# Retention followed by a snake feed-forward layer on one core: the third tile's mask, mix and copies in two halves, VectorE's small tables placed later, the fourth tile turned one piece later

## The chip, the core and the metric

The kernel runs on one core of a Trainium2 chip. The metric is the device time of one execution in microseconds (us), lower is better. Several runs of a kernel are given as a median with the lowest and the highest.

The engines are called as in the profile: PE is TensorE (matrix products; PEld is its loading of weights), DVE is VectorE, ACT is ScalarE, POOL is GpSimd, SP is SyncE, which here only issues transfers. DMA transfers are issued by POOL (loads) and SP (transposes and stores) and run beside all engines.

## The reference

Two parts. The first is a retention layer: for every batch (4) and head (8) a 64 x 64 state is decayed and added to at each of 768 steps, and read with the query. The second is a feed-forward layer on the 3072 resulting rows of 512, with the snake function between its two products.

```python
for t in range(S):
    state = gamma[None, :, None, None] * state + einsum('bhd,bhe->bhde', k[:, :, t], v[:, :, t])
    y[:, :, t] = scale * einsum('bhd,bhde->bhe', q[:, :, t], state)
x = y.transpose(0, 2, 1, 3).reshape(B * S, H * D)       # 3072 x 512
h = x @ w_in                                            # 512 -> 2048
s = sin(alpha * h)
out = (h + s * s / (alpha + 1e-9)) @ w_out              # 2048 -> 512
```

## The kernel before, in words

**Tiles.** The 768 steps are cut into 6 chunks of 128. A tile is one chunk of one batch with all 8 heads, so there are 24 tiles. `order` (called `P` further down, L557) puts the first chunk of each of the four batches first; these four tiles are e0, e1, e2 and e3 (L558). They need no state of an earlier chunk. Then come the other chunks, batch by batch: P[4] and P[5] are the second and third chunk of the first batch. The tiles are gathered in 11 groups: the first has the four tiles e0 to e3 (512 rows), each other has two (256 rows).

**What a tile goes through.** It is loaded by POOL's queue, converted to bf16 on the way (L83). Stage T turns q and k on PE against an identity matrix and copies them out of PSUM into `qkT` (`stage_T`, L235; `half_T`, L222, does one of the two and is used for e0 to e2). Stage A multiplies k and q for each head into the PSUM tile `pa` and multiplies the result on DVE by a mask, into `aT` (`stage_A`, L253). For a first chunk the mask is `dec`, which holds the decay as well; for others it is `mask01`, zeros and ones, and the decay is applied by `scale_v` (to v, by the table `kg`) and by the table `qg[:, c]` of the chunk. Stage M multiplies `aT` with v into the PSUM tile `py` (L297), for a later chunk on top of the product with the state (L293), and copies it to the transposed activations `xT` of the group: ACT does it for a first chunk (L301), DVE by a product with `qg` for a later one (L304). `stage_S` (L266) adds to the state, and ACT copies it (`keep_S`, L277).

**The feed-forward layer.** 2048 hidden columns are 16 pieces of 128, called f. A `Slot` (L468) is one piece, or two, for a stretch of rows: PE multiplies `w_in` with `xT` into the PSUM tile `ph` (4 matmuls of a piece, L482), ACT takes the sine into `s` (L485), `sq` squares it on ACT ("A") or DVE ("D"), and `add` puts h + s*s/alpha into `gT` on DVE (L497, with `rec_alpha`). `ff_out` (`F` in the first group) multiplies `gT` with `w_out` (L507) into `po`, one matmul for each piece and each 128 rows.

**What sets the order.** Everything here is under a manual schedule: each engine runs its instructions in the order in which the program writes them, and waits only for the semaphores of what it reads or overwrites. PSUM tiles have tags; a tag has one buffer ("pa", "ps", "ty") or four ("mm"), and a new tile of a tag waits until the readers of the old one are done. The order around the start (L557 to L807) is written out by hand; from L808 on a table places the work of the tiles between the slots of each group.

**The first 50 us.** Loads are issued by POOL in this order: v of e0, then e1, e2, two pieces of `w_in` (four of its f each), and, behind POOL's own `scale_v(e0)` and `decay_table` 2 and 3 (L604 to L606), e3, then the pieces of `w_out` and `w_in` by turns, then P[4], P[5] and so on. `idle_work(n)` (L549) issues n matmuls of 512 columns on a tile of zeros. e0, e1 and e2 go through T, A and M. Then the first 384 rows of group 0 begin their slots, `w[0]`, `w[2]`, `w[1]`, `w[4]`, `w[7]`, `w[6]`, `w[3]`, `w[5]` (`early`, with `w[4]` in the PSUM buffer "ps"), and e3 goes through T, A and M between them. The F matmuls begin with F(1, 0, 2) (the tile e1, pieces 0 and 1), for which the first piece of `w_out` is wanted. Pieces 8 to 15 follow, then the tiles P[4] and P[5], then `phase(1, ...)`, which works on group 1 (P[4] and P[5]). From there to the end the phases follow one another.

**DVE's small tables** that the change moves: `rec_alpha` (L587, L597), `mask01` (L592), `maskq` (`later_mask`, L193: two compares on 64 partitions and a copy; first read at L359), and `qg` of the chunks 1, 4 and 5 (`decay_table`, L205; chunks 2 and 3 are POOL's).

Of the kernel before, what the change touches and what calls it, by code (L numbers as in the profile page):

```python
# [8 lines left out]
F32 = mybir.dt.float32  # L9
BF16 = mybir.dt.bfloat16  # L10
ACTF = mybir.ActivationFunctionType
ALU = mybir.AluOpType
# [3 lines left out]
def kernel(  # L16
# [15 lines left out]
    nc = tc.nc  # L32
    B, H, S, D = q.shape
    C = 128
    NCH = S // C
    NJ = B * NCH
    NP = H // 2
# [15 lines left out]
    place = {j: (g, i) for g, js in enumerate(groups) for i, j in enumerate(js)}  # L53
# [4 lines left out]
    psum = ctx.enter_context(tc.tile_pool(name="psum", bufs=1, space=bass.MemoryType.PSUM))  # L58
# [8 lines left out]
    raw = {}  # L67
# [18 lines left out]
    def wide(j):  # L86
        return j >= NCH + 2 and j % NCH > 0
# [40 lines left out]
    tio = consts.tile([128, C], F32, name="tio")  # L128
    nc.gpsimd.iota(tio, pattern=[[1, C]], channel_multiplier=0, base=0, allow_small_or_imprecise_dtypes=True)
    pos = consts.tile([128, NCH], F32, name="pos")  # L130
# [16 lines left out]
    warm = consts.tile([128, 512], BF16, name="warm")  # L147
    nc.vector.memset(warm, 0.0)  # L148
    tiny = consts.tile([128, 1], F32, name="tiny")
# [10 lines left out]
    dec = consts.tile([128, 2, NP, C], F32, name="dec")  # L160
# [12 lines left out]
    mask01 = consts.tile([128, 128], BF16, name="mask01")  # L173
    mask_bc = mask01[:, None, :].to_broadcast([128, H, 128])
# [18 lines left out]
    def later_mask():  # L193
        for b in range(2):
            nc.vector.tensor_scalar(maskq[64 * b:64 * b + 64, 0:128], tio[64 * b:64 * b + 64],
                                    tok[64 * b:64 * b + 64, 0, 0:1], None, op0=ALU.is_ge)
        nc.vector.tensor_copy(maskq[:, 128:192], maskq[:, 0:64])
# [7 lines left out]
    def decay_table(c, eng):  # L205
        eng.tensor_mul(qg[:, c], qg[:, 0], step[:, c, :, None].to_broadcast([128, NP, C]))  # L206
# [3 lines left out]
    alpha_sb = consts.tile([128, FF], F32, name="alpha_sb")  # L210
    rec_alpha = consts.tile([128, FF], F32, name="rec_alpha")
# [7 lines left out]
    st = {}  # L219
    xT = {}  # L220

    def half_T(j, i, eng):  # L222

        if i == 0:
            st["qkT", j] = work.tile([128, 2 * NP, 128], BF16, name="qkT", tag="qkT", bufs=6)
        pt = psum.tile([128, NP, 128], BF16, name="pt", tag="mm", bufs=4)
        for p in range(NP):
            nc.tensor.transpose(pt[:, p, :], raw["qk"[i], j][:, 2 * p:2 * p + 2, :].rearrange("p h d -> p (h d)"), ident)
        o = st["qkT", j][:, i * NP:(i + 1) * NP, :]
        if eng is nc.scalar:  # L230
            nc.scalar.copy(o, pt)
        else:
            nc.vector.tensor_copy(o, pt)

    def stage_T(j, eng=None, tag="ty"):  # L235
        pt = psum.tile([128, 2 * NP, 128], BF16, name="pt", tag=tag, bufs=4 if tag == "mm" else 1)
        st["qkT", j] = work.tile([128, 2 * NP, 128], BF16, name="qkT", tag="qkT", bufs=6)
        for i in range(2):
            for p in range(NP):
                nc.tensor.transpose(pt[:, i * NP + p, :],  # L240
                                    raw["qk"[i], j][:, 2 * p:2 * p + 2, :].rearrange("p h d -> p (h d)"), ident)
        if eng is nc.scalar:
            nc.scalar.copy(st["qkT", j], pt)
        else:
            nc.vector.tensor_copy(st["qkT", j], pt)
# [4 lines left out]
        nc.sync.dma_start_transpose(out=st["qkT", j], in_=raw["qk", j].rearrange(  # L250
            "i a f p d -> i (a f p d)" if wide(j) else "i a h d -> i (a h d)"))

    def stage_A(j):  # L253
        qkT = st["qkT", j]
        pa = psum.tile([128, 2, NP, 128], F32, name="pa", tag="pa")
        for p in range(NP):
            for e in range(2):
                r = slice(64 * e, 64 * e + 64)
                nc.tensor.matmul(pa[:, e, p, :], qkT[r, NP + p, :], qkT[r, p, :],  # L259
                                 start=(p == 0), stop=True, skip_group_check=True)  # L260
        aT = work.tile([128, 2, NP, 128], BF16, name="aT", tag="aT", bufs=2)
        m = dec.rearrange("p e n t -> p (e n) t") if j % NCH == 0 else mask_bc
        nc.vector.tensor_mul(aT.rearrange("p e n t -> p (e n) t"), pa.rearrange("p e n t -> p (e n) t"), m)  # L263
        st["aT", j] = aT

    def stage_S(j):  # L266
        c = j % NCH
        if c == 0:
            st["ps"] = psum.tile([128, NP, D], F32, name="ps", tag="ps")
        ps = st["ps"]  # L270
        for p in range(NP):
            for e in range(2):
                nc.tensor.matmul(ps[64 * e:64 * e + 64, p, :], raw["k", j][:, 2 * p + e, :], raw["v", j][:, 2 * p + e, :],
                                 start=(c == 0 and p == 0), stop=True, skip_group_check=True)
        return ps

    def keep_S(j, ps):  # L277
        for e in range(2):
            r = slice(64 * e, 64 * e + 64)
            nc.scalar.copy(s_bd[(j % NCH + 1) % 2][r, :, r], ps[r, :, :])  # L280

    def stage_M(j, tag="ty"):
        c = j % NCH
        g, i = place[j]
        if g not in xT:
            xT[g] = work.tile([128, KS, sizes[g] * C], BF16, name="xT", tag="xT", bufs=3)
        qkT, aT, vs = st["qkT", j], st["aT", j], raw["v", j]
        py = psum.tile([128, NP, 128], F32, name="py", tag=tag)
        if c > 0:
            for p in range(NP):  # L290
                for e in range(2):
                    r = slice(64 * e, 64 * e + 64)
                    nc.tensor.matmul(py[r, p, :], s_bd[c % 2][:, p, r], qkT[:, p, :],  # L293
                                     start=(p == 0), stop=True, skip_group_check=True)
        for p in range(NP):
            for e in range(2):
                nc.tensor.matmul(py[64 * e:64 * e + 64, p, :], vs[:, 2 * p + e, :], aT[:, e, p, :],  # L297
                                 start=(c == 0 and p == 0), stop=True, skip_group_check=True)
        x = xT[g][:, :, i * C:(i + 1) * C]
        if c == 0:  # L300
            nc.scalar.copy(x, py)  # L301
            return
        ps = stage_S(j) if c < NCH - 1 else None
        nc.vector.tensor_mul(x, py, qg[:, c])  # L304
        if ps is not None:
            if wide(j + 1):
                swapped(s_b[(c + 1) % 2], ps, nc.scalar.copy)
                swapped(s_f, ps, nc.vector.tensor_copy)
            else:
                keep_S(j, ps)  # L310

    def half(x):
        return slice(64 * x, 64 * x + 64)

    def swapped(o, ps, copy):

        m = NP // 2
        copy(o[:, :m], ps[:, :m])  # L320
        for e in range(2):
            copy(o[half(1 - e), m:], ps[half(e), m:])
# [226 lines left out]
    def idle_work(n):  # L549
        for _ in range(n):  # L550
            nc.tensor.matmul(spare["ps"], warm[:, :128], warm, start=True, stop=True)  # L551

    def grow(p):
        nc.scalar.activation(out=qg[:, 0, p, :], in_=tio, func=ACTF.Exp, scale=lgp[:, p:p + 1], bias=cscale)
# [3 lines left out]
    e0, e1, e2, e3 = P[:B]  # L558
# [14 lines left out]
    grow(0)  # L573
    idle_work(2)
    stage_A(e0)
    grow(1)
    half_T(e1, 0, nc.scalar)
# [5 lines left out]
    nc.scalar.copy(alpha_sb, pal)  # L583
    stage_M(e0)
    stage_A(e1)
    idle_work(2)
    nc.vector.tensor_scalar_add(rec_alpha, alpha_sb, 1e-9)  # L587
    grow(3)
    half_T(e2, 0, nc.scalar)
    idle_work(2)  # L590
    half_T(e2, 1, nc.vector)
    nc.vector.tensor_scalar(mask01, tio, pos[:, 0:1], None, op0=ALU.is_ge)  # L592
    stage_M(e1)
    nc.scalar.activation(out=tiny, in_=warm[:, 0:1], func=ACTF.Sin)
    idle_work(1)
    stage_A(e2)
    nc.vector.reciprocal(rec_alpha, rec_alpha)  # L597
    later_mask()
    decay_table(1, nc.vector)
    idle_work(6)  # L600
    stage_M(e2)
    idle_work(3)

    scale_v(e0, nc.gpsimd)  # L604
    decay_table(2, nc.gpsimd)
# [54 lines left out]
    def F(ts, lo, hi):  # L660
        for f in range(lo, hi):
            ff_out(0, ts, f)

    def early(f, tag="mm"):
        return Slot(0, f, (0, n3), tag=tag)

    w = {}
    decay_table(4, nc.vector)
    w[0] = early(0)
    w[0].sq("D")  # L670
    w[2] = early(2)
# [5 lines left out]
    w[1].add()  # L677
    w[7] = early(7)
    w[2].add()
    stage_T(e3, nc.vector, "ty")  # L680
    w[7].sq("A")
    w[6] = early(6)
    decay_table(5, nc.vector)
    w[6].sq("A")
    stage_A(e3)
    w[4].sq("A")
# [77 lines left out]
    F(1, 8, 9)  # L764
    w[13].sq("A")
    w[10].add()
    F(0, 6, 8)
    w[14] = Slot(0, 14)
    F(2, 0, 1)
# [4 lines left out]
    F(0, 9, 10)  # L774
    w[14].sq("A")
    w[13].add()
    F(0, 10, 12)
    w[15] = Slot(0, 15)
    F(2, 2, 3)
    w[12].add()  # L780
    w[14].add()
    w[15].sq("A")
    F(2, 3, 4)
    F(2, 4, 6)
    F(0, 12, 13)
    stage_T(P[4], nc.vector, "pa")
    F(0, 13, 15)
    w[15].add()
    F(1, 10, 12)
    stage_A(P[4])  # L790
    F(0, 15, 16)
# [9 lines left out]
    scale_v(P[5], nc.vector)  # L801
    F(2, 7, 11)
    stage_M(P[4])
    F(2, 11, 16)
    stage_M(P[5])
    stage_T(P[6], nc.vector, "mm")
# [66 lines left out]
```

## Time and profile before

| | |
|---|---|
| median of 3 runs | 212.47 us (211.97 to 213.03) |
| the profiled execution | 212.53 us |
| its span, first to last instruction | 210.8 us |
| granted TensorE clock | 1.000 |
| busy: PE, DVE, ACT, POOL | 200.8, 156.9, 157.4, 108.4 us |
| first slot of the feed-forward layer starts on PE | 15.29 us |
| first F matmul starts on PE | 24.01 us |
| first matmul of phase 1 starts on PE | 48.20 us |

A row of a timeline is: start in us, time it took in us, engine, line, operation, what is written and read, how many instructions of the kind were merged into the row, and, in brackets, how long the engine had been idle before it and what ended that. "L507" is line 507 of the kernel. A matmul's row ends some 0.16 us after PE has begun the next one, since the matmuls are pipelined; starts tell more than ends. A row of a DMA gives the time that POOL took to issue it; the time to landing is given apart.

### The profile page before, as it was taken

Reading aid. Unit: us, or ns where it says so; the run is one execution under the profiler, and the core shown is the slowest. Engines: PE = TensorE matmul, PEld = TensorE weight load, DVE = VectorE, ACT = ScalarE, POOL = GpSimd, SP = SyncE. Lnnn points to the kernel's source line nnn. Section 1 sums busy time; section 2 is a strip of 40 time slices with the busy share of each in tenths; the row PEclk is TensorE's granted clock in tenths of the full one; section 3 lists DMA queues with packets and bytes.
Section 4 is the critical chain, followed back from the end, with each engine's and each line's share of the span. In section 5 each row is a group of like instructions: output and inputs, shape, how many; then the busy total and the mean of one; then the engine's idle time right before and its main releaser. Section 6 shows DMA issues by size and latency. Waiting matters only on the chain.

```text
span 210.8 us, 5640 instructions
## 1 busy us (share of the span) xinstructions
PE 200.8 (95%) x2252; PEld 132.0 (63%) x2278; DVE 156.9 (74%) x348; ACT 157.4 (75%) x337; POOL 108.4 (51%) x143
## 2 busy tenths in 40 slices
PE   7998899999999999999999999999999999999994
PEld 3544554557766666667667666666666666666653
DVE  7797985777988687787797777778777768686540
ACT  7767798458998877877877877876876786888821
POOL 8898433898895929999989941000222020000000
PEclk9999999999999999999999999999999999999999
DMA  9999999999999999999999999165123110110113
GB/s 129 153 190 153 191 207 187 154 182 216 122 123 149 154 100 130 161 117 142 151 180 171 162 126 125 62 66 79 63 70 71 54 48 5 50 53 0 50 50 103
DMA packets 100282, 24.76 MB, mean 117 GB/s; under 512 B 92816, under 2 KB 97312, under 8 KB 100256
## 3 DMA queue, kind: packets, MB, share of 16 engines
q0 software_dynamic: 77504, 13.38, 93.5%
q1 hardware_dynamic: 22608, 10.96, 26.9%
q8 instruction: 18, 0.29, 0.6%
q14 instruction: 8, 0.07, 0.1%
q10 hardware_dynamic: 144, 0.07, 0.1%
HBM read 27.27 MB, written 6.29 MB: 159 GB/s over the span
## 4 chain that ended last, share of the span: by engine, by line
PE 87%; DMA 4%; POOL 3%; DVE 2%; issue 2%; ACT 1%; DVEq 0%; POOLq 0%
PE po L507 37%; PE ph L482 36%; DMA w_out<-in_moe_w_out_dram 4%; PE spare L551 3%; PE poh L532 2%; PE py L338 2%; PE py L293 1%; PE pa L259 1%; POOL qg L206 1%; PE pt L240 1%; PE pa L375 1%; PE py L420 1%; POOL qkr L83 1%; PE py L297 1%; PE pa L350 1%
## 5 line engine op out<-in xcount | busy, mean ns | idle before, releaser
L497 DVE SCALAR_TENSOR_TENSOR gT<-s,rec_alpha,ph 128x256 bf16<-128x256 f32 (+3 forms) x184 | 82.1, 489 | 31.6 <-ACT s L490 31.1
L485 ACT ACTIVATE s<-ph,alpha_sb 128x256 f32<-128x256 f32 (+3 forms) x184 | 79.4, 481 | 33.1 <-PE ph L482 32.1
L482 PE MATMUL ph<-xT,w_in 128*128 128x256 bf16 (+3 forms) x735 | 98.8, 277 | 0.1
L507 PE MATMUL po<-w_out,gT 128*128 128x512 bf16 x344 | 90.1, 379 | 4.1 <-issue 2.9
L482 PEld LDWEIGHTS <-w_in 128*128 128x128 bf16 x736 | 70.6, 98 | 30.6 <-DMA w_in<-in_moe_w_in_dram 0.5
L490 ACT ACTIVATE s<-s 128x512 f32<-128x512 f32 (+1 forms) x91 | 56.4, 623 | 2.7
L507 PEld LDWEIGHTS <-gT 128*128 128x128 bf16 x368 | 34.0, 98 | 27.0 <-issue 0.9
L391 POOL CAST s_b<-s_f 128x256 bf16<-128x256 f32 x5 | 2.0, 397 | 42.4 <-DVE s_f L384 24.9
L138 POOL TENSOR_TENSOR v_seq<-v_seq,kgq 128x512 bf16<-128x512 bf16 x14 | 14.6, 1068 | 8.8 <-DMA v_seq<-in_v_dram 8.8
L104 POOL DMA_DIRECT2D qk_seq<-in_q_dram x24 | 17.1, 748 | 2.5 <-DMA vr<-in_v_dram 0.8
L104 POOL DMA_DIRECT2D qk_seq<-in_k_dram x24 | 17.1, 734 | 0.5 <-DMA qk_seq<-in_q_dram 0.4
L519 DVE COPY o_sb<-po 128x512 f32<-128x512 f32 x19 | 13.1, 692 | 5.6 <-PE po L507 5.5
L104 POOL DMA_DIRECT2D v_seq<-in_v_dram x24 | 17.0, 754 | 0.0
L359 DVE TENSOR_TENSOR aTw<-pa,maskq 128x768 bf16<-128x768 f32 x14 | 13.3, 952 | 0.0
L551 PE MATMUL spare<-warm 128*128 128x512 bf16 x28 | 10.1, 486 | 1.4 <-DVE warm L148 1.2
L83 POOL DMA_DIRECT2D vr<-in_v_dram x10 | 9.2, 918 | 3.7 <-DMA w_out<-in_moe_w_out_dram 3.4
L138 POOL TENSOR_TENSOR vr<-vr,kg 128x512 bf16<-128x512 bf16 x8 | 8.6, 1079 | 3.2 <-DMA vr<-in_v_dram 2.6
L83 POOL DMA_DIRECT2D qkr<-in_q_dram x9 | 8.1, 897 | 3.8 <-DMA w_in<-in_moe_w_in_dram 3.6
L83 POOL DMA_DIRECT2D qkr<-in_k_dram x9 | 8.0, 889 | 3.6 <-DMA w_out<-in_moe_w_out_dram 3.1
L443 DVE TENSOR_TENSOR xT<-py,qg 128x256 bf16<-128x256 f32 x26 | 9.7, 416 | 0.0
L263 DVE TENSOR_TENSOR aT<-pa,mask 128x1024 bf16<-128x1024 f32 x6 | 7.3, 1218 | 0.0
L492 DVE TENSOR_TENSOR s<-s 128x512 f32<-128x512 f32 (+1 forms) x7 | 4.4, 633 | 3.7 <-ACT s L485 3.7
(108 smaller groups left out, 154.8 us busy)
## 6 DMA issues: line engine op xcount, KB each, us to landing
out_dram<-o_sb SPq DMA_DIRECT2D x23, 256.0 KB, 2.4
w_in<-in_moe_w_in_dram POOLq DMA_DIRECT2D x4, 512.0 KB, 9.7
w_out<-in_moe_w_out_dram POOLq DMA_DIRECT2D x4, 512.0 KB, 13.9
vr<-in_v_dram POOLq DMA_DIRECT2D x10, 128.0 KB, 6.6
qk_seq<-in_q_dram POOLq DMA_DIRECT2D x16, 80.0 KB, 6.1
qk_seq<-in_k_dram POOLq DMA_DIRECT2D x16, 80.0 KB, 5.1
v_seq<-in_v_dram POOLq DMA_DIRECT2D x16, 80.0 KB, 5.8
qkr<-in_q_dram POOLq DMA_DIRECT2D x9, 128.0 KB, 6.9
```

What stands on the lines that cost most here:

```text
L83: nc.gpsimd.dma_start(out=t, in_=chunk_of(src, j))
L104: nc.gpsimd.dma_start(out=o, in_=src[bt, h, cs[0] * C:, :].rearrange("(f i) d -> i f d", i=64))
L138: eng.tensor_mul(t, t, by[:, j % NCH, :, None].to_broadcast([128, H, D]))
L359: return {"mask": lambda: nc.vector.tensor_mul(aT, pa[:, :, 0:384].rearrange("p e (m t) -> p e m t", m=2), maskq[:, None, None, :].to_broa ...
L443: nc.vector.tensor_mul(x[:, 2 * b:2 * b + 2, :], y.rearrange("p (m t) -> p m t", m=2), qg[:, c, 2 * b:2 * b + 2])
L482: nc.tensor.matmul(self.ph[:, m, :], w_in[:, i, f * 128:(f + 1) * 128], xT[g][:, i, self.lo:self.hi], start=(m == 0 and i == 0), stop=(i = ...
L485: nc.scalar.activation(out=self.s[:, m, :], in_=self.ph[:, m, :], func=ACTF.Sin, scale=alpha_sb[:, f:f + 1])
L490: nc.scalar.activation(out=self.s, in_=self.s, func=ACTF.Square)
L497: nc.vector.scalar_tensor_tensor(gT[self.g][:, f, self.lo:self.hi], self.s[:, m, :], rec_alpha[:, f:f + 1], self.ph[:, m, :], op0=ALU.mult ...
L507: nc.tensor.matmul(po[g, ts], gT[g][:, f, ts * C:(ts + 1) * C], w_out[:, f, :], start=(f == 0), stop=(f == FF - 1))
L519: nc.vector.tensor_copy(o_sb, po[g, ts])
L551: nc.tensor.matmul(spare["ps"], warm[:, :128], warm, start=True, stop=True)
```

## The change

- e2's stage A is called with two parts: the eight matmuls are as before, but DVE's product with `dec` is made in two halves, one for the head pairs 0 and 1, one for 2 and 3.
- e2's stage M is replaced by `halves_M`: four matmuls into a PSUM tile with the tag "ps", copied to `xT` by ACT, two matmuls of `idle_work`, four matmuls into a tile with the tag "ty", copied to `xT` by DVE. Around it `idle_work` is 3 + 2 + 3 instead of 6 + 3.
- The dummy sine of ACT, which loads the table of sines, stands ahead of e1's stage M instead of behind it.
- On DVE, `rec_alpha` (both instructions) and `decay_table(1)` come behind e2's copies; `mask01` goes from ahead of e2's mask to behind `w[10].add()`; `decay_table(4)` and `(5)` go to behind `w[13].add()` and `w[14].add()`; `maskq` goes to behind `stage_M(P[4])`.
- `stage_T(e3)` comes behind the slot `w[6]` instead of ahead of its matmuls.
- `w[15].add()` comes ahead of `stage_T(P[4])` instead of behind it and two F matmuls.

```diff
-    def stage_A(j):
+    def stage_A(j, parts=1):
...
-        m = dec.rearrange("p e n t -> p (e n) t") if j % NCH == 0 else mask_bc
-        nc.vector.tensor_mul(aT.rearrange("p e n t -> p (e n) t"), pa.rearrange("p e n t -> p (e n) t"), m)
+        flat = "p e n t -> p (e n) t"
+        if parts > 1:
+            for h in range(0, NP, NP // parts):
+                r = slice(h, h + NP // parts)
+                nc.vector.tensor_mul(aT[:, :, r], pa[:, :, r], dec[:, :, r])
+        else:
+            nc.vector.tensor_mul(aT.rearrange(flat), pa.rearrange(flat), dec.rearrange(flat) if j % NCH == 0 else mask_bc)
...
+    def halves_M(j):
+        g, i = place[j]
+        aT, vs = st["aT", j], raw["v", j]
+        for h, (tag, copy) in enumerate((("ps", nc.scalar.copy), ("ty", nc.vector.tensor_copy))):
+            idle_work(2 * h)
+            py = psum.tile([128, 2, 128], F32, name="py", tag=tag)
+            for n in range(2):
+                for e in range(2):
+                    p = 2 * h + n
+                    nc.tensor.matmul(py[64 * e:64 * e + 64, n, :], vs[:, 2 * p + e, :], aT[:, e, p, :],
+                                     start=(n == 0), stop=True, skip_group_check=True)
+            copy(xT[g][:, 2 * h:2 * h + 2, i * C:(i + 1) * C], py)
...
     idle_work(2)
-    nc.vector.tensor_scalar_add(rec_alpha, alpha_sb, 1e-9)
     grow(3)
     half_T(e2, 0, nc.scalar)
     idle_work(2)
     half_T(e2, 1, nc.vector)
-    nc.vector.tensor_scalar(mask01, tio, pos[:, 0:1], None, op0=ALU.is_ge)
+    nc.scalar.activation(out=tiny, in_=warm[:, 0:1], func=ACTF.Sin)
     stage_M(e1)
-    nc.scalar.activation(out=tiny, in_=warm[:, 0:1], func=ACTF.Sin)
     idle_work(1)
-    stage_A(e2)
+    stage_A(e2, 2)
+    idle_work(3)
+    halves_M(e2)
+    idle_work(3)
+    nc.vector.tensor_scalar_add(rec_alpha, alpha_sb, 1e-9)
     nc.vector.reciprocal(rec_alpha, rec_alpha)
-    later_mask()
     decay_table(1, nc.vector)
-    idle_work(6)
-    stage_M(e2)
-    idle_work(3)
...
     w = {}
-    decay_table(4, nc.vector)
     w[0] = early(0)
...
     w[2].add()
-    stage_T(e3, nc.vector, "ty")
     w[7].sq("A")
     w[6] = early(6)
-    decay_table(5, nc.vector)
+    stage_T(e3, nc.vector, "ty")
     w[6].sq("A")
     stage_A(e3)
...
     w[10].add()
+    nc.vector.tensor_scalar(mask01, tio, pos[:, 0:1], None, op0=ALU.is_ge)
     F(0, 6, 8)
...
     w[13].add()
+    decay_table(4, nc.vector)
     F(0, 10, 12)
     w[15] = Slot(0, 15)
     F(2, 2, 3)
     w[12].add()
     w[14].add()
+    decay_table(5, nc.vector)
     w[15].sq("A")
     F(2, 3, 4)
     F(2, 4, 6)
     F(0, 12, 13)
+    w[15].add()
     stage_T(P[4], nc.vector, "pa")
     F(0, 13, 15)
-    w[15].add()
     F(1, 10, 12)
     stage_A(P[4])
...
     stage_M(P[4])
+    later_mask()
     F(2, 11, 16)
     stage_M(P[5])
```

## The prediction

> **What bounds the kernel now.** I read the page first (the shares, then the chain that ended last), then the timeline of PE up to 50 us, the landing of each early load, and the timelines of DVE and POOL beside them.
>
> ```profile
> span 210.8 us, 5640 instructions
> PE 200.8 (95%) x2252; PEld 132.0 (63%) x2278; DVE 156.9 (74%) x348; ACT 157.4 (75%) x337; POOL 108.4 (51%) x143
> PE 87%; DMA 4%; POOL 3%; DVE 2%; issue 2%; ACT 1%; DVEq 0%; POOLq 0%
> ```
>
> PE bounds it. The 4% of DMA is one piece: the chain has 8.49 us of the first piece of w_out, 15.47 to 23.97, ahead of the first F matmul. From there PE is on the chain nearly all the time. So there are two regions: up to 24 us (as it will turn out, 34 us) loads set the time, and afterwards PE does, with DVE at a few places.
>
> ```profile
> 14.55 0.82 PE L551 MATMUL spare<-warm 128*128 128x512 bf16 x3
> 15.29 3.67 PE L482 MATMUL ph<-xT,w_in 128*128 128x384 bf16 x20
> 19.69 0.80 PE L240 MATMUL pt<-ident,qkr 128*128 128x128 bf16 x8 [0.73 <-DMA qkr<-in_q_dram]
> 20.33 0.81 PE L482 MATMUL ph<-xT,w_in 128*128 128x384 bf16 x4
> 21.28 0.40 PE L259 MATMUL pa<-qkT 64*128 64x128 bf16 x8
> 21.61 1.47 PE L482 MATMUL ph<-xT,w_in 128*128 128x384 bf16 x8
> 23.01 0.41 PE L297 MATMUL py<-aT,vr 128*64 128x128 bf16 x8
> 24.01 1.02 PE L507 MATMUL po<-w_out,gT 128*128 128x512 bf16 x3 [0.58 <-DMA w_out<-in_moe_w_out_dram]
> ```
>
> The reader is to see PE stopped twice by a load, at 19.69 for e3's q and at 24.01 for w_out. Issue plus time to landing, asked for one load at a time, gives: w_in piece 0 7.66 + 7.2 = 14.9; piece 1 8.4 + 9.0 = 17.4 (the weight loads of PE wait 0.5 us for w_in at one place); e3's k 13.74 + 6.3 = 20.0; w_out 0 15.47 + 8.5 = 24.0; w_in 2 16.22 + 10.3 = 26.5; w_out 1 16.95 + 12.1 = 29.0; w_in 3 17.68 + 14.2 = 31.9; w_out 2 18.42 + 15.8 = 34.2; w_out 3 19.93 + 16.8 = 36.7. The pieces of 512 KB land 2.3 to 3 us apart throughout (three loads of 128 KB lie ahead of w_out 0): a full line, not a late issue, sets these times. F(1, 8, 9) is the first to need w_out 2, and PE starts it at 34.22, 0.22 us after its last slot matmul was through.
>
> **The front, part by part (11 to 34 us).** DVE loses rec_alpha (0.72) and mask01 (0.80) from between e1's product and e2's.
>
> ```profile
> 2.05 0.43 DVE L164 TENSOR_SCALAR ident<-tio,pos 128x128 bf16<-128x128 f32 x1
> 11.16 0.72 DVE L587 TENSOR_SCALAR rec_alpha<-alpha_sb 128x16 f32<-128x16 f32 x1
> 12.12 0.80 DVE L592 TENSOR_SCALAR mask<-tio,pos 128x128 bf16<-128x128 f32 x1
> 12.85 1.21 DVE L263 TENSOR_TENSOR aT<-pa,dec 128x1024 bf16<-128x1024 f32 x1
> 10.81 2.03 POOL L206 TENSOR_TENSOR qg<-qg,step 128x512 f32<-128x512 f32 x2
> ```
>
> e2's copy of k then starts when its transposes end, 11.4 instead of 11.79, stage A at 12.0 instead of 12.26, the product at about 12.45 instead of 12.85. In halves it takes more: a 512-wide product out of PSUM is 0.69 (xT<-py,qg), so two are 1.38 for 1.21, but the first is out at 13.1. Four matmuls of M follow at 13.2, two spares (0.43), then at 13.85, behind the second half, the other four. DVE's 256-wide copy, 0.4 by the 0.37 of ACT's casts of that width and DVE's 0.69 for 512, ends at 14.6; ACT's half starts once the moved table load (1.28) and e1's copy are done, 13.5, and ends earlier. The spares fall from 10 to 9, 0.22 less. PE could start the slots at 14.65 instead of 15.29. But w_in 0 lands at 14.9, so it starts there: 0.4 earlier. Then three slots (12 matmuls, 1.95 us) bring it to 16.85, and the fourth needs w_in 1, 17.4. The 0.4 is gone there. Next `w[4]`, `w[7]` and the moved `w[6]` end near 19.45; e3's turn waits for q and k as before (19.69, 20.0), its DVE copy ends at 21.2 as before, stage A starts at 21.28 as before. `w[6]` merely went from behind the turn to ahead of it: the 0.73 us wait shrinks and one of the same size opens between turn and A. decay_table(5) (0.68) leaves the gap in which DVE waits for A anyway. M(e3) at 23.0 and F at 24.01 stay. **Sum of the front: 0.** Its cover is the loads: 0.55 us at 16.85, and then 0.6 us at 24.0 and 0.2 at 34.2. If the line of loads were not there, the gain would be 0.4 to 0.65.
>
> **34 to 41 us, what comes back.** The tables land here. mask01 at 34.2 (0.3 to 0.8) and decay_table(4) at 36.1 (0.68) fit in gaps in which DVE waits for ACT (0.98 to 1.27 us each): 0. decay_table(5) does not.
>
> ```profile
> 37.16 1.41 DVE L497 SCALAR_TENSOR_TENSOR gT<-s,rec_alpha,ph 128x512 bf16<-128x512 f32 x2 [0.98 <-ACT s L490]
> 39.82 0.69 DVE L245 COPY qkT<-pt 128x1024 bf16<-128x1024 bf16 x1 [1.25 <-PE pt L240]
> 40.43 0.74 DVE L497 SCALAR_TENSOR_TENSOR gT<-s,rec_alpha,ph 128x512 bf16<-128x512 f32 x1
> 41.09 1.22 DVE L263 TENSOR_TENSOR aT<-pa,mask 128x1024 bf16<-128x1024 f32 x1
> ```
>
> Now: adds of w[12] and w[14] to 38.57, idle, copy of P[4]'s turn 39.82 to 40.52, add of w[15] 40.43 to 41.17; PE makes A(P[4]) at 40.58 and waits 0.25 us for that add, F(0, 15, 16) at 41.23. Then: decay_table(5) 38.5 to 39.2; the add of w[15] when its square is done (ACT ends it at 39.65), 39.68 to 40.43; only then the copy, 40.35 to 41.04. A(P[4]) starts at 41.10, 0.52 later, takes 0.33, and F(0, 15, 16) starts at 41.44: **+0.2**. The wait on the add is gone, a longer one on the copy is in its place. Behind it PE is dense, so the 0.2 stays; P[4]'s product, P[5]'s copy (43.4, A(P[5]) at 43.44, another 0.03) and the two scalings shift by 0.3 to 0.4 and have that cover.
>
> **46 to 48 us, maskq.** It is put between the xT products of P[4] and P[5].
>
> ```profile
> 45.41 0.69 DVE L304 TENSOR_TENSOR xT<-py,qg 128x512 bf16<-128x512 f32 x1
> 47.35 0.69 DVE L304 TENSOR_TENSOR xT<-py,qg 128x512 bf16<-128x512 f32 x1 [1.25 <-PE py L297]
> 46.45 1.09 POOL L138 TENSOR_TENSOR vr<-vr,kg 128x512 bf16<-128x512 bf16 x1
> 14.14 0.83 DVE L195 TENSOR_SCALAR maskq<-tio,tok 64x128 bf16<-64x128 f32 x2
> 15.01 0.49 DVE L197 COPY maskq<-maskq 128x64 bf16<-128x64 bf16 x1
> ```
>
> xT of P[4] ends at 46.35, xT of P[5] could start at 47.58 (47.35 + 0.23) and end at 48.27; PE, through with its turns, wants it at 48.43 (48.20 + 0.23). So the three have 1.25 us and there are 0.1 us behind them. Undisturbed they take under 0.9: nothing. But two rows above show compares that last as long as POOL's product: mask01, of the same shape as `ident`, took 0.80 against 0.43 and ended at 12.92, POOL's second qg at 12.84; rec_alpha, 16 wide, took 0.72, to 11.88, where the first qg ends. So here the second compare (from 46.55) would wait for POOL's product, which ends near 47.6; copy (0.1 to 0.49) until 47.85 to 48.2; xT until 48.55 to 48.9; PE starts 0.15 to 0.5 late. Bounds: 0, if the compares don't wait, and 1.3, if each of the three waits for a POOL instruction (below). I take **+0.3**, the middle of what those rows give for one wait.
>
> The Trainium skill, "SBUF — State Buffer", section "Who interferes with whom", says that copies and tensor_scalar in VectorE's two-port modes hold a port pair shared with GpSimd for a whole instruction, and that the later one blocks. The two rows agree; by that rule the 0.3 stands, and without it this place would cost 0 and the sum be 0.2.
>
> **Sum.** 0 + 0.2 + 0.3 = +0.5 us on the profiled execution's 212.53 us (1.7 of it outside the span): 213.0. The median shown, 212.47, is 0.06 lower, which changes nothing. After 48 us PE starts are dense to the end, so a shift there stays. A measurement of this kernel (211.97 to 213.03) tells about 0.5%, 1.06 us, from no change.
>
> **Rivals.**
> 1. maskq slips through between POOL's instructions: only +0.2, 212.75. For it: the second compare of L195 took 0.28 while POOL was issuing a load. Chance 0.2.
> 2. It gains: the loads come earlier in runs than in this profile, or w[15]'s square ends before decay_table(5) matters. Price: 0.4 of the front, or the 0.3 at 41.23; 212.0 to 212.2. Against it: execution and median agree within 0.06, and the loads are a full line. Chance 0.13. Both together would be 0.9, still under 1.06; more than that needs something I don't see, 0.04.
> 3. The other side: maskq is caught three times. POOL follows its product with issues of 0.7 us from 47.44 on; were the three to end with the product (47.6) and two issues (48.2, 48.9), xT ends at 49.6 and PE starts phase 1 1.2 late: with the 0.2, 214.0. It decides from the point where maskq's copy ends after 47.7; L197's 0.49, which ends with an issue of POOL at 15.50, speaks for it, the 0.28 above against. Chance 0.15.
> 4. PE cools. Its spares took 0.45 each at the start (3.59 for 8) and 0.22 later. The waits between 16.8 and 24 are regrouped: 0.55, 0.25, 0.95, 0.6. At half speed the 2.4 us of matmuls there and some 3 us behind would cost about 2.5: 215.0. Before has waits of 0.25, 0.75, 0.3 and 0.6 there and stays fast. Chance 0.03.
>
> The Trainium skill, "TensorE: Matmul & The Clock Gate", section "The HAM clock gate (the "warmup" mystery)", puts the fall back to half rate behind an idle window of about 3.4 us; by that rule rival 4 does not happen, as no wait here comes near it.
>
> **Chances.** Forecast 213.0 (by itself 212.7 to 213.4) 0.45; rival 1 0.2, 2 0.13, more gain 0.04, 3 0.15, 4 0.03. Faster 0.04; within 0.5% 0.45 + 0.2 + 0.13 = 0.78; slower 0.18. The range, 212.0 to 214.0, leaves out what lies beyond rivals 2 and 3.
>
> **What would show it.** Right: slots start near 14.9 and pause for w_in near 17.4; F starts at 24.0 and 34.2 as now; A(P[4]) at 41.1 behind the copy; a compare of L195 over 0.5 us at 46.5; phase 1 at 48.7. Wrong: F at 24.01 moves with the front, or phase 1 starts before 48.2.

## The result, and the profile after

The changed kernel takes 213.36 us (median of 10 runs, 212.66 to 213.74), the kernel before, in 10 runs, 212.05 us (211.81 to 213.03). The ratio is 1.0045, 95% interval 1.0028 to 1.0062: slower by 0.6 to 1.3 us. The forecast was 213.0. The profiled execution of the changed kernel took 213.03 us, 0.50 more than that of before. This 0.50 can be followed step by step; what the medians show beyond it cannot, and is taken up at the end of the experiments. The two profiled executions do not lie alike among the runs: that of before, 212.53, is longer than eight of its ten, that of the changed kernel, 213.03, shorter than seven of its ten. So the 0.50 is less than the medians differ by.

From the page of the changed kernel:

```profile
span 211.3 us, 5639 instructions
PE 200.4 (95%) x2251; PEld 132.1 (63%) x2277; DVE 157.3 (74%) x350; ACT 157.1 (74%) x337; POOL 108.2 (51%) x143
...
PE 86%; DMA 5%; POOL 3%; issue 2%; DVE 1%; ACT 1%; POOLq 0%
PE ph L501 39%; PE po L526 36%; DMA w_in<-in_moe_w_in_dram 5%; PE poh L551 2%; POOL qkr L83 2%; PE py L357 2%; POOL vr L83 1%; PE pa L259 1%; PE py L298 1%; PE pt L240 1%; PE pa L394 1%; PE pa L369 1%; PE py L439 1%; PE py L302 1%; DVE qkT L245 1%
```

PE bounds it as before. The DMA piece on the chain is now w_in instead of w_out: the second piece, issued at 8.39, landed at 18.9. The changed kernel's lines are numbered 19 higher from its `Slot` on: L501 is L482 of before, L526 is L507. Its timeline of PE, the rows that answer to those of before:

```profile
15.36 2.12 PE L501 MATMUL ph<-xT,w_in 128*128 128x384 bf16 x12 [0.26 <-DMA w_in<-in_moe_w_in_dram]
18.97 2.12 PE L501 MATMUL ph<-xT,w_in 128*128 128x384 bf16 x12 [1.48 <-DMA w_in<-in_moe_w_in_dram]
20.93 0.61 PE L240 MATMUL pt<-ident,qkr 128*128 128x128 bf16 x8
22.32 0.40 PE L259 MATMUL pa<-qkT 64*128 64x128 bf16 x8 [0.79 <-DVE qkT L245]
...
24.06 0.41 PE L302 MATMUL py<-aT,vr 128*64 128x128 bf16 x8
24.40 1.04 PE L526 MATMUL po<-w_out,gT 128*128 128x512 bf16 x3
...
34.40 0.81 PE L526 MATMUL po<-w_out,gT 128*128 128x512 bf16 x3
...
41.28 0.40 PE L259 MATMUL pa<-qkT 64*128 64x128 bf16 x8 [0.44 <-DVE qkT L245]
41.61 0.61 PE L526 MATMUL po<-w_out,gT 128*128 128x512 bf16 x2
...
48.68 1.03 PE L501 MATMUL ph<-xT,w_in 128*128 128x256 bf16 x8
```

The reader is to see four times, each against before. F(1, 0, 2) starts at 24.40 (24.01), F(1, 8, 9) at 34.40 (34.22), F(0, 15, 16) at 41.61 (41.23), phase 1 at 48.68 (48.20). So the lateness is 0.39, then 0.18, 0.38, 0.48; the end of the span is 0.50 later. Of the 0.39 a part is given back, because before waited for w_out 2 at 34.22 (it landed at 34.17 in both kernels) and the changed kernel does not. Then two additions follow, 0.20 and 0.10.

DVE around the second and the third of these, and POOL beside it:

```profile
38.67 0.68 DVE L206 TENSOR_TENSOR qg<-qg,step 128x512 f32<-128x512 f32 x1
39.87 0.75 DVE L516 SCALAR_TENSOR_TENSOR gT<-s,rec_alpha,ph 128x512 bf16<-128x512 f32 x1 [0.51 <-ACT s L509]
40.53 0.68 DVE L245 COPY qkT<-pt 128x1024 bf16<-128x1024 bf16 x1
...
45.79 0.69 DVE L309 TENSOR_TENSOR xT<-py,qg 128x512 bf16<-128x512 f32 x1
46.40 1.42 DVE L195 TENSOR_SCALAR maskq<-tio,tok 64x128 bf16<-64x128 f32 x2
47.85 0.23 DVE L197 COPY maskq<-maskq 128x64 bf16<-128x64 bf16 x1
47.94 0.69 DVE L309 TENSOR_TENSOR xT<-py,qg 128x512 bf16<-128x512 f32 x1
```

```profile
46.34 1.09 POOL L138 TENSOR_TENSOR vr<-vr,kg 128x512 bf16<-128x512 bf16 x1
```

The copy of P[4]'s turn waits for the add of w[15], and A(P[4]) for the copy. The two compares of maskq take 1.42 us together; the first alone 1.12, to 47.52, POOL's product ending at 47.43. P[5]'s xT ends at 48.63, 0.05 us ahead of phase 1.

### The profile page after: what moved, and what is told of

Its sections match the earlier page's. It is cut to its first block, busy times and chain, and to the rows that moved or that the text cites. A ratio compares the mean times of both kernels' runs of the same rounds, so it can differ in the third digit from the quotient of the medians.

```text
span 211.3 us, 5639 instructions
## 1 busy us (share of the span) xinstructions
PE 200.4 (95%) x2251; PEld 132.1 (63%) x2277; DVE 157.3 (74%) x350; ACT 157.1 (74%) x337; POOL 108.2 (51%) x143
## 4 chain that ended last, share of the span: by engine, by line
PE 86%; DMA 5%; POOL 3%; issue 2%; DVE 1%; ACT 1%; POOLq 0%
PE ph L501 39%; PE po L526 36%; DMA w_in<-in_moe_w_in_dram 5%; PE poh L551 2%; POOL qkr L83 2%; PE py L357 2%; POOL vr L83 1%; PE pa L259 1%; PE py L298 1%; PE pt L240 1%; PE pa L394 1%; PE pa L369 1%; PE py L439 1%; PE py L302 1%; DVE qkT L245 1%
## 5 line engine op out<-in xcount | busy, mean ns | idle before, releaser
L501 PE MATMUL ph<-xT,w_in 128*128 128x256 bf16 (+3 forms) x735 | 98.6, 277 | 1.8 <-DMA w_in<-in_moe_w_in_dram 1.7
L526 PE MATMUL po<-w_out,gT 128*128 128x512 bf16 x344 | 90.1, 379 | 3.2 <-issue 2.9
L501 PEld LDWEIGHTS <-w_in 128*128 128x128 bf16 x736 | 70.6, 98 | 32.5 <-DMA w_in<-in_moe_w_in_dram 2.6
L526 PEld LDWEIGHTS <-gT 128*128 128x128 bf16 x368 | 34.0, 98 | 25.8
```

The lines of the kernel that those rows point to most:

```text
L501: nc.tensor.matmul(self.ph[:, m, :], w_in[:, i, f * 128:(f + 1) * 128], xT[g][:, i, self.lo:self.hi], start=(m == 0 and i == 0), stop=(i = ...
L526: nc.tensor.matmul(po[g, ts], gT[g][:, f, ts * C:(ts + 1) * C], w_out[:, f, :], start=(f == 0), stop=(f == FF - 1))
```

## The experiments

**Theory A** is the prediction's: the front gives nothing, since loads bound it; the time is lost behind 34 us, where the copy waits for w[15] and maskq waits for POOL. **Theory B**: the front itself costs, because with `w[6]` gone from behind e3's turn PE waits for the copy of it (the 0.79 above). Its variant B2, formed after the first four runs: the new front makes w_in land late.

Single runs lie up to 0.65% below and 1% above the median of their kernel, so the edits are told apart by two lengths in the profiles: how long behind the landing of w_out 0 F(1, 0, 2) starts, and from F(1, 8, 9) to phase 1. Before has 0.04 and 13.98 us, the changed kernel 0.39 and 14.28. Much of the spread lies ahead of these lengths: F(1, 8, 9) starts 0.04 to 0.23 us behind the landing of w_out 2, and that was anywhere from 33.1 to 35.0 us. Before and "before again", the same kernel, differ by 0.69 us there and by 0.67 in their spans. "Apart" is how long behind w_in 1 the load of w_out 0 lands.

| kernel | ratio (95%) | w_in 1 lands | apart | F(1, 0, 2) behind w_out 0 | F(1, 8, 9) | phase 1 behind that |
|---|---|---|---|---|---|---|
| before | | 17.4 | 6.52 | 0.04 | 34.22 | 13.98 |
| changed | 1.0045 (1.0028 to 1.0062) | 18.9 | 5.09 | 0.39 | 34.40 | 14.28 |
| w15 back | 1.0029 (1.0011 to 1.0046) | 17.7 | 5.25 | 0.24 | 33.19 | 14.96 |
| turn back | 1.0027 (1.0007 to 1.0047) | 18.6 | 5.08 | 0.05 | 33.84 | 14.30 |
| tables back | 1.0013 (0.9995 to 1.003) | 18.2 | 5.09 | 0.39 | 33.68 | 14.18 |
| front only | 1.0022 (1.0002 to 1.0043) | 18.4 | 5.33 | 0.05 | 34.52 | 13.99 |
| three undone | 0.9994 (0.997 to 1.0017) | 18.2 | 5.08 | 0.04 | 33.45 | 13.98 |
| before, w15 first | 1.001 (0.9985 to 1.0036) | 17.3 | 5.85 | 0.04 | 33.37 | 14.18 |
| before, turn later | 1.0011 (0.9988 to 1.0033) | 17.3 | 6.33 | 0.04 | 33.79 | 13.98 |
| before, 3 spares more | 1.0048 (1.0023 to 1.0073) | 18.0 | 5.09 | 0.05 | 33.33 | 13.98 |
| before again | 0.9987 (0.9964 to 1.0009) | 18.2 | 5.08 | 0.04 | 33.53 | 13.98 |
| before, maskq late | 1.0021 (1.0001 to 1.004) | 18.2 | 6.63 | 0.04 | 35.05 | 14.23 |
| before, F swapped | 1.0003 (0.998 to 1.0026) | 16.8 | 7.54 | 0.05 | 34.55 | 13.77 |
| before, 3 spares less | 1.0001 (0.9982 to 1.002) | 17.9 | 6.07 | 0.09 | 34.12 | 13.99 |

### The changed kernel with one part undone

w15 back:

```diff
-    w[15].add()
     stage_T(P[4], nc.vector, "pa")
     F(0, 13, 15)
+    w[15].add()
```

> The changed kernel with one order undone: w[15].add() again behind P[4]'s turn and F(0, 13, 15). Theory A (VectorE's new order behind 34 us costs the time: P[4]'s copy waits for the add of w[15]): F(0, 15, 16) starts about 0.2 us earlier against the first slot matmuls before it, and the ratio to before falls from 1.0045 by 0.001 to 0.002, to about 1.003. Theory B (the front costs it: with one slot less behind the turn of e3, TensorE waits there when the second piece of w_in lands late): no change, 1.0045.

F(0, 15, 16) again starts 0.64 behind A(P[4]) with the wait of 0.25 for the add, as before, and A(P[4]) no longer waits for the copy. But phase 1 came later, not earlier. PE, DVE and POOL of this kernel ahead of it:

```profile
46.56 1.07 PE L240 MATMUL pt<-ident,qkr 128*128 128x128 bf16 x16
48.15 1.03 PE L501 MATMUL ph<-xT,w_in 128*128 128x256 bf16 x8 [0.52 <-DVE xT L309]
```

```profile
45.28 2.01 DVE L195 TENSOR_SCALAR maskq<-tio,tok 64x128 bf16<-64x128 f32 x2
47.32 0.18 DVE L197 COPY maskq<-maskq 128x64 bf16<-128x64 bf16 x1
47.41 0.68 DVE L309 TENSOR_TENSOR xT<-py,qg 128x512 bf16<-128x512 f32 x1
```

```profile
45.21 0.91 POOL L83 DMA_DIRECT2D vr<-in_v_dram  x1
46.10 1.09 POOL L138 TENSOR_TENSOR vr<-vr,kg 128x512 bf16<-128x512 bf16 x1
```

Here both compares were held: the first to 46.17, when POOL's issue of a load ended (46.12), the second to 47.29 (product 47.19). That cost 0.69 us on PE: from the first of the 16 matmuls of the turns to phase 1 it is 1.59 here and 0.90 in before (the 0.52 in brackets begins at the end of the turns' row). So maskq's price depends on what POOL does in the 2 us beside it. Another 0.27 went to P[5]'s k, not yet landed when its turn began; the edit touches no load. The ratio, 1.0029, is what theory A expected, though this execution does not show it.

Turn back:

```diff
+    stage_T(e3, nc.vector, "ty")
     w[7].sq("A")
     w[6] = early(6)
-    stage_T(e3, nc.vector, "ty")
```

> The changed kernel with one order undone: e3's turn again ahead of the slot w[6]. Theory A: the loads cover it, F(1, 0, 2) starts where it did within 0.1 us, ratio 1.0045 as the changed kernel. Theory B: the 0.79 us wait between turn and stage A is filled by the slot again, M(e3) comes up to 0.5 us earlier where w_in lands late, and the ratio falls to about 1.002.

w_in 1 landed late here too (18.6), and yet M(e3) was through in time and F(1, 0, 2) started 0.05 behind its load: theory B is right for this part. F was in time although the loads lay only 5.08 apart. In the three kernels with both the new front and the later turn (changed, w15 back, tables back) F starts 5.48 behind w_in 1, with the loads 5.09 to 5.25 apart. The rest, 14.30, is that of the changed kernel, as theory A has it. PE of this kernel:

```profile
18.60 1.47 PE L501 MATMUL ph<-xT,w_in 128*128 128x384 bf16 x8 [1.24 <-DMA w_in<-in_moe_w_in_dram]
19.91 0.78 PE L240 MATMUL pt<-ident,qkr 128*128 128x128 bf16 x8
20.53 0.81 PE L501 MATMUL ph<-xT,w_in 128*128 128x384 bf16 x4
21.48 0.40 PE L259 MATMUL pa<-qkT 64*128 64x128 bf16 x8
...
23.68 1.02 PE L526 MATMUL po<-w_out,gT 128*128 128x512 bf16 x3
```

The slot of four matmuls again lies between turn and A, and PE hardly waits for the copy.

Tables back (mask01, maskq and decay tables 4 and 5 where they were before; the rest as changed; of the edit, maskq is shown):

```diff
     nc.vector.reciprocal(rec_alpha, rec_alpha)
+    later_mask()
...
     stage_M(P[4])
-    later_mask()
```

> The changed kernel with mask01, maskq and decay tables 4 and 5 again at the places they had before; halves, spares, turn and the early add of w[15] stay. Theory A: most of the cost is the add of w[15] ahead of the copy, which stays, so it moves by 0.1 us (maskq) at most: ratio 1.004; phase 1 starts about 0.1 us earlier than with the tables late. If the tables themselves are the cost, it falls to 1.001. Theory B: no change either.

14.18: 0.10 less than the changed kernel, 0.20 more than before. The 0.20 is the add of w[15], the 0.10 maskq, as theory A had it. The time does not agree with that: theory A expected 1.004, and the ratio is 1.0013, its interval ending at 1.003, near the 1.001 that was to stand for the tables as the main cost. "Three undone" below keeps mask01 and decay tables 4 and 5 late and loses nothing, so if a table costs more over many runs than the 0.10 of this profile, it is maskq.

Front only (the kernel before with the new front, its tables, turn and add of w[15] as they were; a part of the edit, against before):

```diff
-    stage_A(e2)
+    stage_A(e2, 2)
+    idle_work(3)
+    halves_M(e2)
...
-    idle_work(6)
-    stage_M(e2)
```

> Before with the front of the change alone: halves, table load of ScalarE, 9 spares, rec_alpha and decay table 1 behind e2; turn, add of w[15] and the other tables as before. Both theories: the slots are ready earlier by up to 0.6 us, the landing of w_in takes it back, F(1, 0, 2) starts at the landing of w_out: ratio 1.000 within 0.0015. If the loads were not the limit, 0.997.

In its profile PE waits 0.60 us for w_in 0, 0.39 for w_in 1 and 0.33 for w_out 0; both lengths are those of before. So the halves gain nothing and cost nothing there. The ratio, 1.0022, is above what was expected, at most 1.0015, and its interval leaves out 1. The next run has the same front, but for the tables, and 0.9994, so this may be spread; it was not shown.

### All three undone, and single parts added to before

Three undone (the two edits above, and `later_mask` behind P[5]'s xT; new front, late mask01 and late decay tables stay):

```diff
     stage_M(P[4])
-    later_mask()
     F(2, 11, 16)
     stage_M(P[5])
+    later_mask()
```

> The changed kernel with the add of w[15] and e3's turn back at their places and maskq behind P[5]'s xT; the new front and the late mask01 and decay tables 4, 5 stay. Theory A (VectorE's order behind 34 us is the cost): ratio 1.000 to 1.001, and phase 1 starts 13.9 to 14.0 us behind F(1, 8, 9) as before. Theory B2 (something of the new front delays the loads: the second piece of w_in landed at 17.7 to 18.9 in five profiles with the new front against 17.4 before): ratio stays at 1.002 and w_in 1 lands at 17.7 or later.

Time and both lengths are those of before, and the interval lies wholly below that of the changed kernel. Within it the whole loss lies in these three places. mask01 and the decay tables, which stayed late, cost nothing.

Before, with the add of w[15] first:

```diff
+    w[15].add()
     stage_T(P[4], nc.vector, "pa")
     F(0, 13, 15)
-    w[15].add()
```

> Before with one edit: w[15].add() ahead of P[4]'s turn. Theory A: A(P[4]) about 0.5 later, F(0, 15, 16) 0.2 later, ratio 1.001; phase 1 starts 14.2 us behind F(1, 8, 9) instead of 14.0. Theory B2: ratio 1.000 to 1.001 as well, but w_in 1 lands near 17.4 with the old front.

14.18, +0.20, and the wait moves from the add to the copy:

```profile
40.24 0.40 PE L259 MATMUL pa<-qkT 64*128 64x128 bf16 x8 [0.44 <-DVE qkT L245]
40.57 0.61 PE L507 MATMUL po<-w_out,gT 128*128 128x512 bf16 x2
```

Decay table 5 is in its old place here, so it has no part in the 0.20.

Before, with e3's turn later:

```diff
-    stage_T(e3, nc.vector, "ty")
     w[7].sq("A")
     w[6] = early(6)
     decay_table(5, nc.vector)
+    stage_T(e3, nc.vector, "ty")
```

> Before with one edit: e3's turn behind the slot w[6]. Theory A: the loads cover it, ratio 1.000, F(1, 0, 2) at the landing of w_out 0. Theory B: TensorE idles 0.8 us between turn and stage A; M(e3) comes up to 0.5 later and F(1, 0, 2) up to 0.4 later where w_in lands late, ratio up to 1.002. Theory B2: w_in 1 near 17.4.

PE idled 1.07 us ahead of A(e3), and F(1, 0, 2) still started with its load, which left it 0.54 to wait: the loads lay 6.33 apart. By the 5.48 of the three kernels above, the later turn costs when they lie closer than that; this is an estimate. How late w_in 1 lands by itself does not decide it: in "w15 back" it landed at 17.7, earlier than in most, and F was 0.24 late, since w_out 0 came only 5.25 behind.

Before, with three spares more:

```diff
-    idle_work(3)
+    idle_work(6)
```

> Before with three more matmuls of idle_work (0.65 us) behind e2's stage M: the first slot is ready 0.65 later. Theory A (loads bound the front): the slots start near 15.9, w[4] at 17.9 against 17.5, and M(e3) and F(1, 0, 2) move by 0.2 at most: ratio 1.000. If TensorE bounded the front: +0.65, ratio 1.003. Theory B2: w_in 1 near 17.4.

```profile
14.48 1.47 PE L551 MATMUL spare<-warm 128*128 128x512 bf16 x6
15.79 2.11 PE L482 MATMUL ph<-xT,w_in 128*128 128x384 bf16 x12
18.07 1.47 PE L482 MATMUL ph<-xT,w_in 128*128 128x384 bf16 x8 [0.17 <-DMA w_in<-in_moe_w_in_dram]
...
23.16 1.02 PE L507 MATMUL po<-w_out,gT 128*128 128x512 bf16 x4
```

In the profile the loads take the 0.65 us in, as theory A says: the fourth slot starts with w_in 1, F 0.05 behind w_out 0, phase 1 at 47.31. What this execution lost, it lost later: from phase 1 to the end of the span it took 163.78 us, 1.22 more than before (162.56; the changed kernel 162.57), and PE waited at 57 and 81 us for v that POOL had scaled late. "Before, turn later" has 163.16 there, and a wait for such a v at 81. The ratio of 1.0048 is not what theory A expects. By this profile it need not come from the front; whether the edit brings the later waits about stays open.

Before again:

> The kernel before, unchanged, as if it were an experiment. It says how far a ratio may lie from 1 with no difference at all, and gives a second profile with the old front. Both theories: 1.000 within 0.002. Theory B2 (the new front delays the loads) wants w_in 1 near 17.4 again; if it lands at 18 or later here, the landing is chance.

w_in 1 landed at 18.2 with the old front and no edit at all, 5.08 ahead of w_out 0, so a late landing does not need the new front. That alone does not dispose of theory B2. In the six profiles with the new front w_in 1 landed at 18.3 on average and the loads lay at most 5.33 apart in every one; in the eight with the old front it landed at 17.6 on average, and they lay closer than 5.48 in two. w_out 0 itself did not land later with the new front (23.5 on average, against 23.8). Whether the new front brings the two loads together stays open. The ratio, 0.9987, shows how far one lies from 1 by itself.

Before, with maskq late (out of the front, and):

```diff
     stage_M(P[4])
+    later_mask()
     F(2, 11, 16)
```

> Before with one edit: maskq between the xT products of P[4] and P[5], as in the change. Theory A, as it now stands (a compare waits until the instruction of GpSimd that runs beside it ends): one or two of the three instructions last about 1.0 us instead of 0.28, P[5]'s xT ends 0.3 to 0.7 late, TensorE waits that long ahead of phase 1, phase 1 starts 14.3 to 14.7 us behind F(1, 8, 9); ratio 1.001 to 1.003. Rival (they slip through): 14.0 us, ratio 1.000.

DVE of this kernel, then POOL:

```profile
46.85 1.57 DVE L195 TENSOR_SCALAR maskq<-tio,tok 64x128 bf16<-64x128 f32 x2
48.45 0.18 DVE L197 COPY maskq<-maskq 128x64 bf16<-128x64 bf16 x1
48.54 0.69 DVE L304 TENSOR_TENSOR xT<-py,qg 128x512 bf16<-128x512 f32 x1
```

```profile
47.22 1.09 POOL L138 TENSOR_TENSOR vr<-vr,kg 128x512 bf16<-128x512 bf16 x1
```

The compares end behind POOL's product (48.3) again, and phase 1 starts 0.25 us later than in before, a little less than the 0.3 to 0.7 expected. Alone, maskq costs 0.25; behind the late copy of the change 0.10, since PE is late by then itself.

Before, with two matmuls swapped:

```diff
-    F(0, 15, 16)
     F(1, 12, 13)
+    F(0, 15, 16)
```

> Before with one edit: F(1, 12, 13) ahead of F(0, 15, 16), so that a matmul that needs nothing new fills the wait for the add of w[15]. The 0.25 us wait at F(0, 15, 16) shrinks to about 0.05; phase 1 starts 13.8 us behind F(1, 8, 9) instead of 14.0; ratio 0.999, hardly to be told from 1.

13.77, 0.21 shorter than before: this removes the wait that the change meant by its order of w[15]. No difference can be measured in the time (1.0003), and no version here was measurably faster than before.

Before, with three spares less:

```diff
-    idle_work(3)
```

> Before without the last three matmuls of idle_work (0.65 us): the first slot could start at 14.65. Theory A (loads bound the front): it starts when w_in 0 lands, w[4] when w_in 1 lands, ratio 1.000. If TensorE bounded the front in most executions, as the ratio 1.0048 of the kernel with three spares more may say: ratio 0.997.

The time did not change, but the test is not clean: PE then waited 0.67 us for ACT's copy of e2 and started at 15.72.

**What stays open.** The profiles account for 0.5 us, the interval asks for 0.6 to 1.3. Two of the three places differ between the profiles, maskq from 0.10 to 0.69 and the start of F from 0.24 to 0.39 in kernels with the new front and the later turn, and the ratio of "tables back" points at maskq, so a larger mean is likely; it was not shown. The stretch behind the start of phase 1 differs too, 162.55 to 163.78 us, without a known cause.

## Why the prediction held, and where it did not

- **The loads bound the front: right.** The slots were to start near 14.9 and pause near 17.4. They started at 15.36, with w_in 0 (0.26 waited), and paused until 18.97 for w_in 1. F(1, 8, 9) starts 0.23 behind the landing of w_out 2. The loads also hid that PE was ready for the slots at about 14.94 (the last spares from 14.28, 0.82 less the 0.16 by which rows overlap) instead of 14.65; the second half's matmuls started at 14.05, not 13.85. All this rests on the profiles; the ratio of "before, 3 spares more" is not explained by it.
- **"Sum of the front: 0": too low by 0.18.** The step that failed is the one on e3's turn: "`w[6]` merely went from behind the turn to ahead of it", with 0.6 us of cover at 24.0. The cover was counted from one execution, in which w_out 0 landed 6.52 us behind w_in 1. The two lay 5.08 to 7.54 apart in 14 profiles. With the later turn, turn, copy and A follow each other with no slot to fill the 0.95 between turn and A, and F started 5.48 behind w_in 1 in the three kernels with the new front and the later turn. In the changed kernel the loads lay 5.09 apart: M(e3) starts at 24.06 instead of 23.01, and F is 0.39 late, 0.18 behind 34 us. The sign that the prediction named for being wrong, that F at 24.01 moves with the front, came, with F later and not earlier.
- **The add of w[15] ahead of the copy, +0.2: right**, 0.19 to 0.20 in four kernels, by the mechanism named (a wait of 0.44 on the copy in place of 0.25 on the add).
- **maskq, +0.3: right in kind, too high in this execution.** The compare of 1.12 us beside POOL's product is there (the first of the two, not the second), so rival 1 falls. On PE it cost 0.10 in the changed kernel, 0.25 alone and 0.69 where both compares were held for long, by an issue and by the product; that is like rival 3, which had three holds. xT ended at 48.63, inside the 48.55 to 48.9 that were worked out; but PE, 0.18 later than forecast by the turn, wanted it only at 48.58 instead of 48.43. The two misses have one cause and cancel, so the sum, 0.18 + 0.20 + 0.10 = 0.48, agrees with the +0.5 better than its terms do. That is luck.
- **The time, 213.0: near, and partly by luck.** The +0.5 was added to an execution of 212.53 us. The ten runs of before have a median of 212.05; from there the sum gives 212.55, which is below every run of the changed kernel (212.66 to 213.74). Against the 0.6 to 1.3 of the interval, +0.5 is too small.
- **mask01 and decay tables 4 and 5, 0: right.** mask01 took 0.28 at its new place, against 0.80.
- **Rival 2 (a gain) and rival 4 (PE cools) did not come.** Behind the wait of 1.48 us the 384-wide matmuls keep their pace: 12 in 2.12 us, as those at 15.36. The 0.9 for both gains of rival 2 does not follow from its 0.4 and 0.3, which make 0.7.

The Trainium skill, "SBUF — State Buffer", section "Who interferes with whom", was, beside two rows of before, the ground for giving maskq a price. The runs agree with its rule that the second instruction waits until the first has ended: compares of 0.28 us ended 0.09 to 0.10 us behind POOL's product in three kernels.

## What to carry to other kernels

Cover that lies between the landings of two loads is worth their smallest distance over several profiles, not what one profile shows; before a stretch of work is taken out of such a gap, ask what fills it when the load in front comes late. When two results of one engine are due close together, the one that the bound engine reaches first in its own order goes first, however long the other has been ready to start. Small instructions that were moved "out of the way" are priced at their new place by what runs beside them there.

## What was not expected of the hardware

- The same load, issued at 8.4 to 8.6 us behind the same loads, landed between 16.8 and 18.9 us in 14 profiles.
- A compare of VectorE (0.28 us undisturbed) lasted 0.89 us, to 46.17, beside GpSimd's mere issue of a load, which ended at 46.12 (w15 back); in "before, maskq late" one of 0.45 ended at 47.29 and an issue at 47.25. Not every issue does this: in the kernel with three parts undone two compares took 0.57 us together beside issues of other loads, and in the changed kernel mask01 took 0.28 from 34.49, beside an issue of the same form that lasted from 34.46 to 35.33. What decides it is not shown.
